# Attention with a gated convolution: two narrow score blocks in one run, and half-width products sorted by width

## The chip, the cores and the metric

One core of one Trainium2 chip runs the kernel. The metric is the device time of one execution in microseconds (us). Over three runs the kernel before takes 2233.45 to 2233.79 us, with a median of 2233.68 us.

## The reference

Eight batches, each with 3200 rows; `u` and `v` have 256 columns, `z` has 64.

```python
scores = scale * np.matmul(z, z.transpose(0, 2, 1))     # scale = 1/3200
attn = np.maximum(scores, 0.0) ** 2
x = u * np.matmul(attn, v)
gate_pre = sum(conv_w[k] * xp[:, k:k + S, :] for k in range(5))   # causal, per channel
out = (1 / (1 + np.exp(-gate_pre)) * (x @ w_val)) @ w_out
```

The score matrix is symmetric: query and key are both `z`. So a block of scores, once computed, serves a second time when it is turned over.

## The kernel before

**Precision.** Every matrix product is made of three products of 32-bit "r" operands: each operand is split into a high part and a low remainder, and high x low, low x high and high x high are summed in PSUM. For the attention weights the high part is a tile `ah` (a cast, on ACT nearly everywhere) and the remainder a tile `al` (a subtraction, on DVE). There are four buffers of each.

**Side by side.** All large products contract over 64 rows at a time: the upper and the lower half of TensorE's rows each get a list of matmuls, and `side_by_side` (L421 to L433) issues one from each list in turn. The text calls two such matmuls a *pair*. A pair with 512 moving columns is called wide, one with 256 narrow.

**Tiles and steps.** A batch has 25 tiles of 128 rows. As queries they form six chunks of four tiles (c = 0 to 5) and one last single tile, called ONE; as keys they form 12 pairs of tiles and a single one, `SINGLE`. A *step* is one chunk of queries against one pair of keys, so that chunks 0 to 4 have 13 steps (positions 0 to 12) and chunk 5, into which the three steps of ONE are mixed, has 16. A step's key pair is *computed* (scores by TensorE, then on ACT a relu, L651, and a square, L652) or *fetched*: read back from DRAM, where an earlier chunk has stored the turned block. `MIRRORED_AT` fixes at which positions the fetched ones stand. With `F` fetched, `c` computed, `1` the single key tile and `H` the block that is half computed and half fetched, the positions of batches 1 to 7 are

```
chunk 0  ccccccccccc1H        chunk 3  cFccFcFcF1FHF
chunk 1  ccccFcccFcc1H        chunk 4  cFccFFFFFF1FH
chunk 2  ccccFcFcFcF1H        chunk 5  1FcFFSFFFSFHSFFF   (S is a step of ONE; batch 7: 1FcSFSFSHFFFFFFF)
```

In batch 0 only chunks 2 to 5 have an `H`.

**The order on TensorE** is written out by hand in the main loop. In each step s it issues: the first half of the step's attention product (`attend(..., 0)`, six wide pairs, three for the single key tile); then the scores of the step three later (`AHEAD = 3`), if these are computed; then what `filling` has for the step; and then the second half (`attend(..., 1)`). Between the two halves the two row halves swap their accumulators. If a step has neither scores nor filling, its second half is put off (`left`) until a step that has some: then all the second halves that were put off follow one another. `lacks(s)` says that there are no scores for the step three later. A computed block of 512 queries and two key tiles is three wide pairs. The single key tile (`1`) and the half block (`H`) are three narrow pairs each, in a PSUM buffer of their own (`s0` and `s1`, taken in turn by `s_bank`).

**Weights.** At the end of step s, `weights_of` (L609 to L672) issues relu, square and cast on ACT and the subtraction on DVE for step s + 3; for `H` these are L625, L626, L632 and L637, for the others L651, L652, L655 and L663. The new `ah` and `al` take the buffers of step s - 1, so they wait for that step's second half.

**ONE's products.** For the last single tile of queries the roles are swapped (`swap_list`): the weights are stationary and `v` moves. For each of the 25 key tiles there is one wide pair (`ah` against both parts of `v`) and one narrow pair (`al` against the high part). Steps S carry eight key tiles each, issued in two pieces of eight pairs, in the step itself and in the next one; K, the `1` of chunk 5, carries one. The pieces go through `filling`.

Of the kernel before, what the change touches and what calls it, by code (L numbers as in the profile page):

```python
# [12 lines left out]
P = 128  # L13
# [4 lines left out]
def attn_glu_kernel(  # L18
# [40 lines left out]
    n_chunks = NT // 4  # L59
    ONE = n_chunks  # L60
    sizes = [4] * n_chunks + [1]
    firsts = [4 * c for c in range(n_chunks + 1)]
    homes = [(c, t) for c, n in enumerate(sizes) for t in range(n)]
    CW = 4 * P
# [3 lines left out]
    AHEAD = 3  # L68
# [198 lines left out]
    def tiles(c, i):  # L267

        return (GROUP * i, GROUP) if c == ONE else pairs[i]

    def two_pairs(b, c):

        return c < n_chunks and (b > 0 or c > 1)

    def own(c, x):
        return 2 * c + x

    SINGLE = NP - 1
# [12 lines left out]
    def mirrored(b, c, i):  # L291
        k, n = tiles(c, i)
        return all(keeps(b, homes[t][0], c) for t in range(k, k + n))
# [8 lines left out]
    steps, starts = [], {}  # L302
# [26 lines left out]
    N = len(steps)  # L329
# [94 lines left out]
    def side_by_side(upper, lower):  # L424


        ins = None
        for i in range(max(len(upper), len(lower))):
            for r, mms in zip(rows, (upper, lower)):
                if i < len(mms):  # L430
                    out_, st, mv, first, last = mms[i]
                    ins = nc.tensor.matmul(out_, st[r], mv[r], start=first, stop=last)  # L432
        return ins  # L433
# [22 lines left out]
    st_, at = {}, {}  # L456
# [14 lines left out]
    def scores(b, c, i, terms=range(3)):  # L471
        if not terms:
            return
        k, n = tiles(c, i)
        w = sizes[c] * P
        if (b, c, i) not in st_:
            st_[b, c, i] = s_bank()
            if b == c == i == 0:
                apart0.append(ps.tile([P, 512], F32, name="acc1", bufs=1))
        s = st_[b, c, i]  # L480

        q = zt[b, c]
        if halves(b, c, i):
            q, w = q[:, :, w // 2 :], w // 2
        if both(c, i):
            q, w = z_last[b], w + P
        each = w // 2 if n == 1 else w
        sides = []
        for j in range(2):
            g, t = homes[k + (0 if n == 1 else j)]  # L490
            ks = slice(t * P, (t + 1) * P)
            qs = slice(j * each, (j + 1) * each) if n == 1 else slice(0, each)
            kk = zt[b, g]
            mms = []
            for m in terms:
                kp, qp = (((0, 0), (0, 1), (1, 0)) if b == c == i == 0 else ((0, 1), (1, 0), (0, 0)))[m]
                bank = apart0[0] if b == c == i == 0 and j else s[:, j]
                mms.append((bank[:, :each], kk[:, kp, ks], q[:, qp, qs], m == 0, m == 2))
            sides.append(mms)
        side_by_side(*sides)  # L500

    def both(c, i):
        return c == n_chunks - 1 and i == SINGLE
# [7 lines left out]
    def halves(b, c, i):  # L511
        return two_pairs(b, c) and i == own(c, 1)
# [189 lines left out]
    def swap_list(b, c, i, bank):  # L702

        if b not in swaps:
            held_s[0] = next_s[0]
            swaps[b] = ps.tile([P, 2, 512], F32, name=f"s{held_s[0]}", bufs=1)
            swapped[b] = 0
        out_ = swaps[b][:, bank]
        if c == ONE:
            k, n = tiles(c, i)  # L710
            ah, al = (x[:, : n * P].rearrange("p (j x) -> p j x", j=n) for x in at[b, c, i])
        else:
            k, n, w = NT - 1, 1, sizes[c] * P
            ah, al = (x[:, w : w + P].rearrange("p (j x) -> p j x", j=1) for x in at[b, c, i])
        mms = []
        for j in range(n):
            both_v = vt[b, (k + j) // 2][:, :, (k + j) % 2]
            first = swapped[b] + j == 0
            last = swapped[b] + j == NT - 1
            whole = (out_.rearrange("p (x d) -> p x d", x=2), ah[:, j], both_v, first, last)  # L720
            half = (out_[:, :D], al[:, j], both_v[:, 0], False, False)
            mms += [whole, half] if first else [half, whole]
        return mms

    def swap(b, c, i, piece=0, pieces=1):

# [597 lines left out]

    def lacks(s):

        return s + AHEAD >= N or mirrored(*steps[s + AHEAD])

    PIECES = {
# [27 lines left out]
    def fill_at(s, fn, *args):  # L1357
        filling.setdefault(s, []).append((fn, *args))
# [48 lines left out]
    for b in range(B):  # L1407
        for c in range(n_chunks + 1):
            s0 = start(b, c)
            met = start(b, 0) + firsts[c] // 2 - AHEAD  # L1410
            if b == 0:
                met -= c == 1
                at_step(-AHEAD - 4 if c == 2 else met - 5, z_load, b, c)
                if c in (1, 2):
                    at_step(-AHEAD - 2, z_double, b, c)
                early = 1 if c == 0 else -1 if c == 3 else 0
                if c != 1:
                    at_step(met - 3 - early, z_turn, b, c)
                    at_step(met - 2 - early - (c == 3), z_high, b, c)
                    at_step(met - 1 - early - (c >= 2) - (c == 3), z_low, b, c)  # L1420
            else:
                s1 = Z_FROM[b][c] + start(b, 0)
                at_step(s1, z_load, b, c)
                late = 1 if b == 1 else 0
                at_step(s1 + late + 3, z_turn, b, c)
                at_step(s1 + late + 4, z_high, b, c)
                at_step(s1 + late + 5, z_low, b, c)
            if c == ONE:
                continue
            nxt = start(*divmod(b * n_chunks + c + 1, n_chunks))  # L1430
            nb, nc_ = divmod(b * n_chunks + c + 1, n_chunks)
            for h in range(DH):
                for part in range(2):
                    at_step(max(s0 + U_LOAD[b > 0][c], 2) + 2 * h + part, u_load, b, c, h, part)
            if (b, c) != LAST:
                for r, fn, args in BEHIND:
                    r -= b == c == 0 and fn is x_low
                    late = b == c == 0 and fn in (gate_value, gate_value_high, gate_value_low)
                    if late:
                        r = min(r + FIRST_VALUE - VALUE, FIRST_LAST[r])  # L1440
                        if fn is not gate_value_low and args == (1,):
                            r, args = (r - 1, (1, "zz")) if fn is gate_value else (r - 1, args)
                    elif fn in (gate_value, gate_value_high, gate_value_low):
                        r = GATE.get(max(value_places(nb, nc_), default=VALUE), {}).get(r, r)
                    at_step(nxt + r, fn, b, c, *args)
                ends = project_places(nb, nc_)
                for x in range(DH):
                    at_step(nxt + (2 if len(ends) > 1 else project_at(nb, nc_) + 1 + x), out_copy_before, b, c, x)
                if b or c:
                    at_step(nxt + 5, out_unpark, *divmod(b * n_chunks + c - 1, n_chunks))  # L1450
            at_step(max(s0 + U_PREP[b > 0][c], 6), u_prep, b, c)
        for s in range(start(b, 0), start(b + 1, 0)):
            if mirrored(*steps[s]) or halves(*steps[s]):
                sooner = steps[s][:2] == (0, n_chunks - 2)
                at_step(s - AHEAD - FETCH - sooner, m_fetch, *steps[s], first=True)
            if steps[s][1] == ONE:
                for piece in range(2):
                    fill_at(s + piece, swap, *steps[s], piece, 2)
                done = s + 1
            elif both(*steps[s][1:]):  # L1460
                fill_at(s, swap, *steps[s])
        if b < B - 1:
            at_step(done, one_take, b)
        else:
            at_step(done + 1, one_take, b, first=True)
        if b == 0:
            for i in (2, *range(4, NP)):
                at_step(i - 3 + (i == 2), v_high, b, i)
                at_step(i - 2, v_low, b, i)
            for k in (0, 2, 4, 6, 24):  # L1470
                at_step(k // 2 - (5 if k else 7), v_load0, k)
            for g in range(2, 6):
                at_step(firsts[g] // 2 - 5, v_load_chunk, b, g)
        else:
            s1 = start(b - 1, n_chunks - 1)
            for i, p in enumerate(V_HIGH):
                p += b == 1 and p > 13
                at_step(s1 + p, v_high, b, i)
                at_step(s1 + p + 1, v_low, b, i)
            for p, tiles_, place_ in V_LOAD:  # L1480
                p += b == 1 and p > 13
                at_step(s1 + p, v_load_at, b, tiles_, place_)
# [245 lines left out]
```

## Time and profile before

| | |
|---|---|
| median of three runs | 2233.68 us |
| the profiled execution's own time | 2233.61 us |
| its span, first to last instruction | 2231.8 us |
| TensorE (PE) busy | 2227.0 us, 100% of the span, 20083 matmuls |
| VectorE (DVE) busy | 1862.1 us, 83% |
| ScalarE (ACT) busy | 1659.5 us, 74% |
| granted TensorE clock, mean | 1.00 of 2.4 GHz |
| narrow pairs of `H` and `1` scores and of ONE's products | 3 pairs a block; 200 pairs |

The first table of the page gives each engine's busy time. Matmuls overlap in it (a 512-column matmul is shown with 387 ns, while pairs start every 227 ns), so what a run of matmuls costs is read from starts in the timeline: from the start of its first pair to the start of the first pair behind it.

### The profile page before, as it was taken

What the parts mean: (1) busy time and instruction counts of PE and PEld (TensorE: products, weight loads), DVE (VectorE), ACT (ScalarE), POOL (GpSimd) and SP (SyncE); (2) the same over time, 40 slices, a digit from 0 to 9 for tenths busy, and PEclk for the clock granted to TensorE, in tenths of its full rate; (3) what the DMA queues carried; (4) which work ended last, traced back from release to release, by engine and by line L of the source; (5) the groups of instructions that cost most, each with busy time, mean ns of one, the idle gap of its engine ahead of it and who ended that gap; (6) DMA issues with size and microseconds to landing.
All of it is one profiled execution on the core that took longest, in us unless ns stands there. A gap on an engine that the chain in (4) does not pass through costs nothing.

```text
span 2231.8 us, 49169 instructions
## 1 busy us (share of the span) xinstructions
PE 2227.0 (100%) x20083; PEld 1886.7 (85%) x20083; DVE 1862.1 (83%) x2307; ACT 1659.5 (74%) x2038; POOL 87.0 (4%) x131
## 2 busy tenths in 40 slices
PE   9999999999999999999999999999999999999999
PEld 8888888888888888888888888888888888888888
DVE  8978798877888778887889868888788987888777
ACT  8886688766887668876688766877668776687764
POOL 0000000000000000000000000000000000000001
PEclk9999999999999999999999999999999999999999
DMA  6568767886678866788577885778858787587763
GB/s 154 123 143 203 205 154 169 183 200 183 158 171 188 202 176 156 177 190 200 162 177 171 189 207 152 174 177 185 211 145 186 175 185 204 149 182 176 168 179 110
DMA packets 707859, 390.34 MB, mean 175 GB/s; under 512 B 419120, under 2 KB 641328, under 8 KB 707632
## 3 DMA queue, kind: packets, MB, share of 16 engines
q1 hardware_dynamic: 707056, 386.74, 71.6%
q8 instruction: 157, 2.57, 0.5%
q14 instruction: 70, 0.57, 0.1%
q10 hardware_dynamic: 576, 0.46, 0.1%
HBM read 213.53 MB, written 173.54 MB: 173 GB/s over the span
## 4 chain that ended last, share of the span: by engine, by line
PE 95%; ACT 2%; DVE 2%; issue 1%; POOL 0%; DVEq 0%; ACTq 0%; POOLq 0%
PE acc L432 69%; PE s L432 13%; PE misc L432 12%; ACT a L652 1%; DVE turned L524 1%; ACT a L651 1%; PE acc L752 0%; ACT ah L655 0%; DVE al L663 0%; PE acc L747 0%; PE misc L747 0%; PE s L883 0%; PE misc L990 0%; DVE gate L830 0%; PE misc L439 0%
## 5 line engine op out<-in xcount | busy, mean ns | idle before, releaser
L432 PE MATMUL acc<-ah,v_hl 64*128 64x512 f32 x9288 | 1546.4, 387 | 0.0
L432 PEld LDWEIGHTS acc<-ah,v_hl 64*128 64x128 f32 x9288 | 889.3, 184 | 162.3 <-issue 0.3
L432 PE MATMUL acc<-al,v_hl 64*128 64x512 f32 x4644 | 915.6, 387 | 0.1
L663 DVE TENSOR_TENSOR al<-a,ah 128x1024 fp32r<-128x1024 f32 x342 | 392.3, 1147 | 160.1 <-ACT ah L655 159.4
L432 PEld LDWEIGHTS acc<-al,v_hl 64*128 64x128 f32 x4644 | 445.1, 184 | 80.2 <-DVE al L663 1.1
L651 ACT ACTIVATE a<-s 128x1024 f32<-128x1024 f32 x342 | 329.5, 963 | 136.5 <-PE s L432 117.1
L655 ACT CAST ah<-m 128x1024 fp32r<-128x1024 f32 x256 | 266.7, 1045 | 161.4 <-PE acc L432 97.0
L652 ACT ACTIVATE a<-a 128x1024 f32<-128x1024 f32 x342 | 343.5, 1004 | 10.9
L663 DVE TENSOR_TENSOR al<-m,ah 128x1024 fp32r<-128x1024 f32 x256 | 310.1, 1211 | 33.9 <-ACT ah L655 33.9
L524 DVE STREAM_TRANSPOSE turned<-a 128x1024 f32<-128x1024 f32 (+1 forms) x282 | 323.5, 1147 | 0.8 <-DMA mir<-turned 0.8
L655 ACT CAST ah<-a 128x1024 fp32r<-128x1024 f32 (+2 forms) x317 | 313.8, 990 | 13.5 <-PE acc L432 3.5
L830 DVE SCALAR_TENSOR_TENSOR gate<-x,cw,gate 128x512 f32<-128x512 f32 (+1 forms) x392 | 285.5, 728 | 4.4 <-ACT gate L828 0.5
L432 PE MATMUL s<-zhl,zhl 64*128 64x512 f32 x996 | 140.9, 387 | 0.0
L782 DVE TENSOR_TENSOR x<-acc,ut 128x512 f32<-128x512 f32 (+1 forms) x94 | 60.1, 681 | 75.0 <-PE acc L432 68.9
L933 ACT CAST gvh<-gv 128x512 fp32r<-128x512 f32 x94 | 58.4, 621 | 81.1 <-DVE gv L929 81.0
L432 PEld LDWEIGHTS s<-zhl,zhl 64*128 64x128 f32 x996 | 95.5, 184 | 17.4 <-DVE zhl L258 0.3
L834 ACT ACTIVATE gate<-gate 128x512 f32<-128x512 f32 (+1 forms) x98 | 61.0, 622 | 62.1 <-DVE gate L830 61.8
L432 PE MATMUL s<-zhl,zhl_last 64*128 64x512 f32 (+1 forms) x720 | 88.7, 350 | 0.0
L929 DVE TENSOR_TENSOR gv<-misc,gate 128x512 f32<-128x512 f32 x92 | 63.2, 687 | 21.3 <-PE misc L432 17.1
L432 PEld LDWEIGHTS s<-zhl,zhl_last 64*128 64x128 f32 x720 | 66.1, 184 | 11.1
L432 PE MATMUL s<-v_hl,ah 64*128 64x512 f32 x400 | 73.2, 395 | 0.0
L432 PE MATMUL misc<-xh,w_val_lo 64*128 64x512 f32 x368 | 72.3, 386 | 0.0
(245 smaller groups left out, 2099.7 us busy)
## 6 DMA issues: line engine op xcount, KB each, us to landing
mir<-turned SPq DMA_DIRECT2D x468, 256.0 KB, 4.1
m<-mir SPq DMA_DIRECT2D x234, 512.0 KB, 4.9
u_raw<-in_u_dram SPq DMA_DIRECT2D x384, 64.0 KB, 3.6
mir<-turned SPq DMA_DIRECT2D x376, 64.0 KB, 2.2
m<-mir SPq DMA_DIRECT2D x94, 256.0 KB, 4.3
out_dram<-ob SPq DMA_DIRECT2D x180, 128.0 KB, 3.0
v_raws<-in_v_dram SPq DMA_DIRECT2D x25, 512.0 KB, 5.8
z_raw<-in_z_dram SPq DMA_DIRECT2D x180, 64.0 KB, 3.4
```

The lines of the kernel that those rows point to most:

```text
L432: ins = nc.tensor.matmul(out_, st[r], mv[r], start=first, stop=last)
L524: nc.vector.transpose(into[:, t : t + m], src)
L651: nc.scalar.activation(to, src, AF.Relu, scale=scale)
L652: nc.scalar.activation(a, a, AF.Square)
L655: nc.scalar.copy(hi, a)
L663: nc.vector.tensor_tensor(lo, a, f32(hi), op=ALU.subtract)
L782: nc.vector.tensor_tensor(x[:, h, HALO + cols.start : HALO + cols.stop], accs[b, c][h][:, cols] if with_ is None else with_, ut[b, c][:, h ...
L830: nc.vector.scalar_tensor_tensor(g, tap, cw[:, h, k : k + 1], g, op0=ALU.mult, op1=ALU.add)
L834: nc.scalar.activation(g, g, AF.Sigmoid)
L929: nc.vector.tensor_tensor(gv[:, :w], pvs[b, c][e][:, :w], gates[b, c][:, e, :w], op=ALU.mult)
L933: nc.scalar.copy(gvs[b, c][0][:, e, :w], gv_[b, c, e][:, :w])
```

## The change

Three edits.

First, where a chunk has both a `1` and an `H` and is not the last of its batch, `scores` for the `1` now takes one PSUM buffer for both: the `1` fills columns 0 to 255 of its two banks, the `H` columns 256 to 511, and the six narrow pairs are issued in one run, at the place of the `1`. The later step, in which the `H` scores stood, has no scores any more; `lacks` says so, and by the rule above it puts its second half off, if nothing else fills it.

Second, `swap_list` returns all the narrow pairs of a step of ONE ahead of all its wide ones (the other way round for the first step of a batch), where they alternated. As `cut` halves the list, the first piece is then eight narrow pairs and the second eight wide ones.

Third, a step of ONE issues its two pieces one step sooner if the scores that stand in that sooner step are those of an `H`. By the orders above that is the step at position 9 of chunk 5 in batches 0 to 6.

```diff
-        s = st_[b, c, i]
-
+        sides = score_lists(b, c, i, st_[b, c, i], terms)
+        if joined(b, c, i):
+            st_[b, c, own(c, 1)] = st_[b, c, i][:, :, CW // 2 :]
+            for mms, more in zip(sides, score_lists(b, c, own(c, 1), st_[b, c, own(c, 1)], terms)):
+                mms += more
+        side_by_side(*sides)
+
+    def joined(b, c, i):
+        return i == SINGLE and c < n_chunks - 1 and two_pairs(b, c)
...
-            mms += [whole, half] if first else [half, whole]
-        return mms
+            wholes.append(whole)
+            halves.append(half)
+        return wholes + halves if swapped[b] == 0 else halves + wholes
...
-        return s + AHEAD >= N or mirrored(*steps[s + AHEAD])
+        if s + AHEAD >= N:
+            return True
+        b, c, i = steps[s + AHEAD]
+        return mirrored(b, c, i) or (halves(b, c, i) and c < n_chunks - 1)
...
+                sooner = halves(*steps[s - 1 + AHEAD])
                 for piece in range(2):
-                    fill_at(s + piece, swap, *steps[s], piece, 2)
+                    fill_at(s + piece - sooner, swap, *steps[s], piece, 2)
```

(`score_lists` holds what `scores` did before: it makes the two lists of matmuls for one block.)

## Rows read from the trace of the kernel before

**Rows 1.** Page: span; busy us of each engine, share, instructions.
```profile
span 2231.8 us, 49169 instructions
PE 2227.0 (100%) x20083; PEld 1886.7 (85%) x20083; DVE 1862.1 (83%) x2307; ACT 1659.5 (74%) x2038; POOL 87.0 (4%) x131
```
**Rows 2.** Waits of PE: who waited for whom, total us, times, longest.
```profile
PE misc L439 <- POOL zeros L1525: 1.1, 1, 1.1
```
**Rows 3.** Timeline, PE, batch 3, chunk 3: start us, us, instructions merged.
```profile
1003.01 0.53 PE L432 MATMUL s<-zhl 64*128 64x256 f32 x6
...
1008.15 0.86 PE L432 MATMUL s<-zhl 64*128 64x512 f32 x6
1008.83 0.40 PE L432 MATMUL acc<-ah,v_hl 64*128 64x512 f32 x2
```
**Rows 4.** Timeline, PE: six narrow pairs, then five wide ones.
```profile
1283.47 0.28 PE L432 MATMUL misc<-w_out_hi,one_r 64*128 64x256 f32 x2
...
1284.18 0.40 PE L432 MATMUL acc<-ah,v_hl 64*128 64x512 f32 x2
...
1285.34 0.62 PE L432 MATMUL acc<-ah,v_hl 64*128 64x512 f32 x4
```
**Rows 5.** Timeline, PE: twelve narrow pairs, then scores.
```profile
103.45 0.28 PE L432 MATMUL misc<-w_out_hi,gvl 64*128 64x256 f32 x2
...
104.88 0.86 PE L432 MATMUL s<-zhl,zhl 64*128 64x512 f32 x6
```
**Rows 6.** Timeline, PE, batch 3, chunk 5: a piece of eight alternating pairs.
```profile
1088.52 0.28 PE L432 MATMUL s<-v_hl,al 64*128 64x256 f32 x2
...
1089.92 0.40 PE L432 MATMUL acc<-ah,v_hl 64*128 64x512 f32 x2
...
1091.30 0.28 PE L432 MATMUL s<-v_hl,al 64*128 64x256 f32 x2
```
**Rows 7.** Groups by line and shape: count, busy us, mean ns, idle before.
```profile
L432 PE MATMUL s<-v_hl,al 64*128 64x256 f32 x400 | 56.7, 277 | 0.0
```
**Rows 8.** Timeline, DVE, batch 3, chunk 3, up to the subtraction of position 10.
```profile
987.72 1.23 DVE L663 TENSOR_TENSOR al<-a,ah 128x1024 fp32r<-128x1024 f32 x1 [1.87 <-ACT ah L655]
...
1002.90 0.71 DVE L830 SCALAR_TENSOR_TENSOR gate<-x,cw,gate 128x512 f32<-128x512 f32 x1
1003.52 1.22 DVE L663 TENSOR_TENSOR al<-m,ah 128x1024 fp32r<-128x1024 f32 x1
```
**Rows 9.** Timeline, batch 2, chunk 2: a subtraction that ends late.
```profile
663.90 1.18 DVE L663 TENSOR_TENSOR al<-m,ah 128x1024 fp32r<-128x1024 f32 x1
...
665.14 0.19 PEld L432 LDWEIGHTS acc<-al,v_hl 64*128 64x128 f32 x2 [0.20 <-DVE al L663]
...
665.47 0.63 PE L432 MATMUL acc<-ah,v_hl 64*128 64x512 f32 x4
```
**Rows 10.** Timeline, batch 2, chunk 3: subtraction of position 10, scores of step 10.
```profile
727.31 1.22 DVE L663 TENSOR_TENSOR al<-m,ah 128x1024 fp32r<-128x1024 f32 x1
...
733.37 0.84 PE L432 MATMUL s<-zhl 64*128 64x512 f32 x6
```
**Rows 11.** Timeline, batch 1, chunk 0: subtraction of position 10, scores of step 10.
```profile
318.80 1.23 DVE L663 TENSOR_TENSOR al<-a,ah 128x1024 fp32r<-128x1024 f32 x1 [0.21 <-ACT ah L655]
...
322.52 0.84 PE L432 MATMUL s<-zhl 64*128 64x512 f32 x6
```
**Rows 12.** Timeline, batch 3, chunk 3, ACT and DVE: weights of positions 11 and 12.
```profile
1005.33 0.60 ACT L632 CAST ah<-m 128x512 fp32r<-128x512 f32 x1
...
1006.88 1.05 ACT L655 CAST ah<-m 128x1024 fp32r<-128x1024 f32 x1
...
1007.96 1.22 DVE L663 TENSOR_TENSOR al<-m,ah 128x1024 fp32r<-128x1024 f32 x1 [0.62 <-ACT ah L655]
```
**Rows 13.** Timeline, batch 3, chunk 5: subtraction of position 12 and its use.
```profile
1092.28 1.22 DVE L663 TENSOR_TENSOR al<-m,ah 128x1024 fp32r<-128x1024 f32 x1
...
1095.45 0.28 PE L432 MATMUL s<-v_hl,al 64*128 64x256 f32 x2
```

More of the change, by code (lines that the diff above doesn't have):

```diff
@@ L473, in scores @@
             return
-        k, n = tiles(c, i)
-        w = sizes[c] * P
         if (b, c, i) not in st_:
@@ L479, in scores, with score_lists @@
                 apart0.append(ps.tile([P, 512], F32, name="acc1", bufs=1))
-        s = st_[b, c, i]
+        sides = score_lists(b, c, i, st_[b, c, i], terms)
[6 more added lines that the diff above has]
+        return i == SINGLE and c < n_chunks - 1 and two_pairs(b, c)
+    def score_lists(b, c, i, s, terms):
+        k, n = tiles(c, i)
+        w = sizes[c] * P
         q = zt[b, c]
@@ L499, in scores @@
             sides.append(mms)
-        side_by_side(*sides)
+        return sides
     def both(c, i):
@@ L714, in swap_list @@
             ah, al = (x[:, w : w + P].rearrange("p (j x) -> p j x", j=1) for x in at[b, c, i])
-        mms = []
+        wholes, halves = [], []
         for j in range(n):
```

## The prediction

> **What bounds the kernel now.** I read the page first: TensorE is busy for 2227.0 of 2231.8 us [rows 1], and its list of waits has one entry, 1.1 us at the start [rows 2]. So the time is the sum of TensorE's issue times, and a change counts only as far as it makes matmuls issue closer or brings a wait. The other engines matter only through the instant at which they deliver. Next I read the timeline by start times, since busy times of matmuls overlap. A wide pair takes 0.227 us: three from 1008.15 to 1008.83 [rows 3]. At the same rate a narrow one would take 0.113.
>
> **Price of a narrow run.** From 1003.01 to 1008.15 [rows 3] the order of the code puts three narrow pairs and 21 wide ones: second halves of positions 7 and 8 (6 + 6), first halves of 9 and 10 (3 + 6). At the two rates that is 0.34 + 4.76 = 5.10; the rows show 5.14, so a block of three costs 0.04 more than its columns. Where does this sit? Six narrow pairs take 0.71 (1283.47 to 1284.18) against 0.68, 0.03 more, and the five wide ones behind them 1.16 against 1.13, another 0.03 [rows 4]: so a narrow run pays a little in each pair and about 0.03 once, when it goes back to wide. Twelve take 1.43 us, 0.119 each [rows 5]: 0.006 per narrow pair, not growing. A run of three is then 0.02 + 0.03, a bit over what rows 3 show; I take 0.04 for three and 0.006 for each pair beyond. Eight pairs that alternate, with the six wide ones behind, take 2.78 (1088.52 to 1091.30) against 4 x 0.113 + 10 x 0.227 = 2.72: 0.06 for a piece [rows 6].
>
> **The change, part by part.**
>
> *Joining.* Batch 0 joins in chunks 2 to 4, batches 1 to 7 in chunks 0 to 4: 3 + 35 = 38 joins. Two blocks cost 2 x 0.04, one run of six 0.04 + 3 x 0.006 = 0.06. Saved: 0.02 each, **0.7 us** in all (bounds 0.4 to 1.1 by the 0.01 us of the rows).
>
> *Sorting.* 400 narrow matmuls are 200 pairs, 25 a batch [rows 7]; one is in K, whose order stays, and 24 in three steps S, 24 steps in all. Before, a step pays 2 x 0.06 = 0.12. After, a piece of eight narrow pairs pays 0.04 + 5 x 0.006 = 0.07 and a piece of eight wide ones nothing. Saved: 0.05 each, 1.2 us. In eight of them the narrow piece now stands right behind the narrow `H` scores (seven by the sooner step; in batch 7 it stood there already), so one return to wide goes too: 8 x 0.03 = 0.2. Together **1.4 us** (bounds 1.0 to 1.8).
>
> *What costs nothing.* The number and shape of all instructions stay, also of relu, square, cast and subtraction; no DMA is issued elsewhere, so SP's and POOL's queues keep their order, and nothing is moved past them. Buffers alternate as before, with one turn fewer; a joined buffer is next written at the second computed block behind it, two steps or more after the relu of its `H` is issued.
>
> *What comes late.* This is the other side of the account. A second half that is put off lets the next first halves come sooner, and these need their `ah` and `al`. In chunks 0, 1, 2 and 4 one second half (position 9 or, in chunk 4, 8 and 9 together) goes behind the scores of step 10, and position 10's first half comes 1.36 us sooner. In chunk 3 of batches 1 to 7 position 8 now has no scores, position 9 never had any, so the second halves of 7 and 8, 12 pairs, go behind the scores of step 10: position 10 is wanted 2.72 us sooner. (The three narrow pairs that move from step 8 to step 6 cancel.) In batch 3 its first half starts six pairs ahead of the scores of step 10, at 1008.15 - 1.36 = 1006.79 [rows 3]; after, at 1004.07 on the same clock. Its `al` is ready at 1003.52 + 1.22 = 1004.74 [rows 8]. That is 0.67 us too late. Can DVE be sooner? Its last idle time is at 987.72, behind it follow 17 us without a gap [rows 8], and nothing in the change lightens them. What does a late `al` cost? In batch 2 one ends at 663.90 + 1.18 = 665.08; the weight load that waited starts at 665.14 and the pair behind it at 665.47 [rows 9]. From the `al` to that pair are 0.39 us. On time, it would start two pairs after the first of the block, which needs no `al`: 0.45. So 0.06 us of lateness is free, and batch 3 loses 0.61 us here. Batches 1, 3 and 5 have the same order; in 2, 4 and 6 the work of ONE's groups stands in between, and in batch 2 the same `al` ends at 728.53 while its first half starts at 733.37 - 1.36 = 732.01 [rows 10]: 3.48 us of room, 0.76 left. Batch 7 has as much. So 3 x 0.61 = **1.8 us** lost. In the other chunks I looked for less than 1.36 us of room at position 10: batch 1, chunk 0, where `al` ends at 320.03 and is wanted at 322.52 - 1.36 = 321.16 [rows 11]: 0.23 late, 0.17 lost. Sum of stalls **2.0 us** (0 if the casts and subtractions come sooner than on this trace, 4 if as late again).
>
> *The sooner step and the pieces.* ONE's narrow pairs need `al`; position 9's is issued at the end of step 6 and now used in step 8, behind a first half and the `H` scores, which I take as no cost. At position 12, `al` ends at 1093.50 and is used at 1095.45 [rows 13]. Position 10's second half (1.36) now goes behind that use, and the sorting takes about 0.1 more: 0.5 us of room left, no cost; if DVE there is 0.5 us later, it costs what is beyond.
>
> *Sum.* 2233.6 (profiled execution) - 0.7 - 1.4 + 2.0 = **2233.5 us**. The median of the runs shown is 0.07 above the profiled one, so I leave it at that. The gain in issue is given back as waits for DVE.
>
> A rule weighed. Rows 6 and 3 show that a piece of alternating widths costs 0.06 us more than its columns. The Trainium skill, "TensorE: Matmul & The Clock Gate", section "Back-to-back issue gap", gives an isolated warm matmul N / 2.4 + 2.5 ns, by its own columns alone; by that the order of widths would be free and both savings nothing. The trace disagrees, with 2.78 against 2.72 us. What it would make of the time is the case of the free order below.
>
> **The rivals.**
> - *No stall* (the weights come in time): 2233.6 - 2.1 = 2231.5. For it: the slack is 0.7 us in 13 steps' work, and relu and square of `H` can run sooner. Against it: DVE had no gap for 17 us [rows 8].
> - *Slower: the four `ah` buffers run out.* At step 10 of chunk 3 the second halves of 7, 8, 9 and 10 are all open, so positions 11 and 12 wait for theirs. Their casts began at 1005.33 and 1006.88, the latter's subtraction ended at 1009.18 [rows 12]. Pushed by 2.72, less what they had spare, position 12 ends near 1011.5 and is wanted near 1012.2 (one first half behind 11's, which follows 1008.15 by 2.72). Room: 0.7 us. If a buffer is seen as free only one second half (1.36) later, position 12 is 0.6 us late and 11 about 0.1, in batches 1, 3 and 5: 3 x 0.7 = 2.1 more, 2235.6. It decides from 0.7 us of extra delay on.
> - *The order of widths is free*: 2233.6 + 2.0 = 2235.6. Against it stand rows 3 to 6.
> - *The change doesn't do what it says*, if the relu of the `1` has to wait for the `H` in the same buffer: 0.35 us on ACT in 38 places. In chunk 3 the cast of position 10 follows it, but DVE is busy until 1003.52 anyway; elsewhere a few tenths: 2234.
>
> **How the numbers follow.** Forecast 0.5 (2233.5, own range 2232.5 to 2234.5); no stall 0.2 (2231.5); buffers run out 0.17 (2235.6); free order 0.05 (2235.6); late relu 0.08 (2234). A range from 2231.0 to 2235.7 leaves out the tails of the second and third case and holds 8 in 10. A measurement of this kernel tells 0.2%, 4.5 us, from no change. Every case lies within this; only several together go beyond, stalls of twice the size and buffers on one side, savings above their bounds on the other: faster 0.04, same 0.90, slower 0.06.
>
> **What would show it.** In the list of waits TensorE stays near 1 us, but in batches 1, 3 and 5 weight loads `acc<-al` wait for DVE L663 by some 0.6 us, at the first half of chunk 3's position 10, after step 8 has lost its scores. Runs of six narrow score pairs take 0.71 us; ONE's pieces become 0.95 (narrow) and 1.82 (wide) where both took 1.40. On ACT the casts L632 of chunk 3 start about 2.7 us later. It would be wrong if the same stall appears in batches 2, 4 and 6, if position 12 of chunk 3 or of chunk 5 waits, or if the time leaves 2231.0 to 2235.7.

## The result: 0.5% slower, and outside the range

The changed kernel takes 2245.51 us (median of 6 runs, 2243.92 to 2247.08) against 2233.56 us before (6 runs, 2233.20 to 2233.79) on the same chip: ratio 1.0054, 95% interval [1.0043, 1.0064]. The forecast was 2233.5. The profiled execution took 2244.64 us. All lines named below as after's are those of the changed kernel: its L672, L939 and L948 are L663, L929 and L938 before.

The page after, beside [rows 1]: the number of matmuls is the same, and TensorE is 14 us short of its span, where it was 4.8 us short.

```profile
span 2242.9 us, 49210 instructions
...
PE 2228.9 (99%) x20083; PEld 1940.9 (87%) x20083; DVE 1862.9 (83%) x2307; ACT 1658.6 (74%) x2038; POOL 87.2 (4%) x131
```

The waits of TensorE after (who waited for whom, total us, times, longest), beside the single entry of [rows 2]:

```profile
PE misc L432 <- DVE gv L939: 7.2, 4, 1.9
PE misc L439 <- POOL zeros L1539: 1.1, 1, 1.1
PE acc L432 <- DVE al L672: 1.0, 3, 0.3
PE acc L432 <- DVE al L583: 0.8, 1, 0.8
```

Two entries count. `acc <- al`, three times, is the stall that was predicted. `misc <- gv`, four times, is one that the prediction does not have. (`acc <- al` L583 stands at 10.03 us, in the start-up.) The same two stand in the list of the weight loads, which sit in front of the matmuls. It shows a stall in its full length; of the ten waits for `al` three are these, 0.77 us each, and the others are 0.15 to 0.45.

```profile
PEld misc L432 <- DVE gv L939: 8.5, 4, 2.2
PEld acc L432 <- DVE al L672: 4.0, 10, 0.8
```

**The predicted stall**, timeline after, batch 3, chunk 3 (start us, us, engine, line, what; in brackets the idle time and what ended it), beside [rows 8]:

```profile
1006.51 1.22 DVE L672 TENSOR_TENSOR al<-m,ah 128x1024 fp32r<-128x1024 f32 x1
...
1007.78 0.19 PEld L432 LDWEIGHTS acc<-al,v_hl 64*128 64x128 f32 x2 [0.77 <-DVE al L672]
1007.78 0.51 PE L432 MATMUL acc<-al,v_hl 64*128 64x512 f32 x2 [0.34 <-DVE al L672]
1008.12 0.64 PE L432 MATMUL acc<-ah,v_hl 64*128 64x512 f32 x4
```

`al` ends at 1007.73 and the weight load that waited starts 0.05 us later; the pair behind it follows 0.39 after the `al`, as [rows 9] had it.

**The other stall**, the same view after, batch 2, chunk 3:

```profile
728.35 1.22 DVE L672 TENSOR_TENSOR al<-m,ah 128x1024 fp32r<-128x1024 f32 x1
...
728.67 0.39 PE L432 MATMUL acc<-ah,v_hl 64*128 64x512 f32 x2
728.90 0.27 PE L432 MATMUL misc<-w_out_hi,one_r 64*128 64x256 f32 x1
...
729.49 0.69 DVE L948 TENSOR_TENSOR gvl<-gv,gvh 128x512 fp32r<-128x512 f32 x1
730.28 0.69 DVE L939 TENSOR_TENSOR gv<-misc,gate 128x512 f32<-128x512 f32 x1
...
731.03 0.18 PEld L432 LDWEIGHTS misc<-w_out_hi,one_r 64*128 64x128 f32 x1 [2.17 <-DVE gv L939]
731.03 0.38 PE L432 MATMUL misc<-w_out_hi,one_r 64*128 64x256 f32 x1 [1.86 <-DVE gv L939]
731.03 0.50 PE L432 MATMUL misc<-w_out_lo,one_r 64*128 64x256 f32 x2
```

and before:

```profile
729.24 0.69 DVE L929 TENSOR_TENSOR gv<-misc,gate 128x512 f32<-128x512 f32 x1
...
730.59 0.28 PE L432 MATMUL misc<-w_out_hi,one_r 64*128 64x256 f32 x2
```

This is ONE's group product (`one_project`), filled in at position 9 of chunk 3. It writes banks named `misc`; DVE's `gv` multiplication first has to read what the value product of chunk 2, which is issued in chunk 3, left in one of them. One matmul goes out at 728.90, the next waits until `gv` has ended at 730.97. Before, `gv` ended at 729.93 and the product started at 730.59: 0.66 us of room that no list of waits shows. The 12 pairs of positions 7 and 8, put off past the product, bring it 12 x 0.227 = 2.72 us forward: 2.06 too late, and 0.06 from the end of `gv` to the matmul make 2.12. The product resumes 731.03 - 728.90 = 2.13 after it began.

**The clock.** In batch 4 the same stall ends at 1286.23. Busy time by stretch, of batch 4 and then of batch 2 (us; busy us and count per engine; granted clock, DMA share, GB/s):

```profile
core 0: us, PE busy (x) PEld busy (x) DVE busy (x) ACT busy (x) POOL busy (x), PEclk, DMA share, GB/s
1284.20:1286.20 2.00, 0.17 (x3) 0.00 (x0) 1.87 (x3) 1.22 (x3) 0.62 (x1) 1.00 1.21 241
1286.50:1289.80 3.30, 3.30 (x23) 3.30 (x23) 0.00 (x0) 0.00 (x0) 0.00 (x0) 0.50 0.55 116
1289.90:1293.00 3.10, 3.10 (x30) 3.10 (x29) 1.48 (x3) 2.61 (x4) 0.00 (x0) 1.00 1.17 206
...
729.00:731.00 2.00, 0.17 (x3) 0.00 (x0) 1.87 (x3) 1.22 (x3) 0.62 (x1) 1.00 1.19 294
731.10:734.40 3.30, 3.30 (x35) 3.30 (x37) 0.32 (x1) 0.97 (x2) 0.00 (x0) 1.00 0.79 139
```

Behind the stall of batch 4 TensorE gets 0.50, 1.2 of 2.4 GHz, throughout these 3.3 us and has 23 matmuls in them; behind that of batch 2, of the same length, it keeps 1.00 and has 35. The clock's own records have 0.50 from 1286.45, 0.2 us after the stall's end, to 1289.87. Half of these 3.4 us is 1.7, an estimate of the loss; by the starts of the chunks it is 1.6. The mean clock of the six runs is 0.997 to 0.999, and the times spread over 3.2 us where those before spread over 0.6.

**The ledger**, how much later each chunk starts than before in the two profiled executions: chunk 3 of batches 1, 3 and 5 adds 0.66, 0.67 and 0.63; of batches 2, 6 and 7 2.10, 2.11 and 1.89; of batch 4 3.71, which is 2.1 and the clock. Start-up adds 0.68, batch 1 chunk 0 0.23, and all the rest, sorting and joining in the main, takes back 1.7. Sum 11.0: 2233.61 to 2244.64.

### The profile page after: what moved, and what is told of

It is laid out like the page before. It is cut to its first block, busy times and chain, and to the rows that moved or that the text cites. A ratio compares the mean times of both kernels' runs of the same rounds, so it can differ in the third digit from the quotient of the medians.

```text
span 2242.9 us, 49210 instructions
## 1 busy us (share of the span) xinstructions
PE 2228.9 (99%) x20083; PEld 1940.9 (87%) x20083; DVE 1862.9 (83%) x2307; ACT 1658.6 (74%) x2038; POOL 87.2 (4%) x131
## 4 chain that ended last, share of the span: by engine, by line
PE 92%; DVE 4%; DMA 1%; issue 1%; ACT 1%; SPq 1%; DVEq 0%
PE acc L432 65%; PE s L432 13%; PE misc L432 12%; DVE al L672 1%; DVE turned L533 1%; DMA mir<-turned 1%; DVE gate L840 1%; PE acc L762 0%; SPq L557 0%; DVE ut L781 0%; PE acc L757 0%; PE misc L757 0%; DVE gv L939 0%; DMA v_raw<-in_v_dram 0%; DMA out_dram<-ob 0%
## 5 line engine op out<-in xcount | busy, mean ns | idle before, releaser
L432 PEld LDWEIGHTS acc<-ah,v_hl 64*128 64x128 f32 x9288 | 928.6, 184 | 137.9 <-issue 0.5
L432 PE MATMUL acc<-al,v_hl 64*128 64x512 f32 x4644 | 940.1, 387 | 1.9 <-DVE al L672 1.0
L432 PEld LDWEIGHTS acc<-al,v_hl 64*128 64x128 f32 x4644 | 469.0, 184 | 72.1 <-DVE al L672 4.0
L672 DVE TENSOR_TENSOR al<-a,ah 128x1024 fp32r<-128x1024 f32 x342 | 392.1, 1146 | 148.2 <-ACT ah L664 146.4
L672 DVE TENSOR_TENSOR al<-m,ah 128x1024 fp32r<-128x1024 f32 x256 | 309.8, 1210 | 32.7 <-ACT ah L664 32.7
L646 DVE TENSOR_TENSOR al<-m,ah 128x512 fp32r<-128x512 f32 x46 | 31.8, 692 | 69.9 <-ACT ah L641 69.1
L939 DVE TENSOR_TENSOR gv<-misc,gate 128x512 f32<-128x512 f32 x92 | 63.2, 687 | 22.0 <-PE misc L432 17.8
```

The lines of the kernel that those rows point to most:

```text
L646: nc.vector.tensor_tensor(l, src, f32(h), op=ALU.subtract)
L672: nc.vector.tensor_tensor(lo, a, f32(hi), op=ALU.subtract)
L939: nc.vector.tensor_tensor(gv[:, :w], pvs[b, c][e][:, :w], gates[b, c][:, e, :w], op=ALU.mult)
```

## Experiments

Two theories besides the waits (W): that a join costs by itself, in the long narrow run or the shared buffer (J); that the sorting or the sooner step costs (S). Beside the first four runs the kernel before takes 2233.56 us, beside the next four 2233.40, beside the last 2233.47; ratios are to these.

**Sorting and sooner step without the joins**

```
 def joined(b, c, i):
-    return i == SINGLE and c < n_chunks - 1 and two_pairs(b, c)
+    return False
...
-    return mirrored(b, c, i) or (halves(b, c, i) and c < n_chunks - 1)
+    return mirrored(b, c, i)
```

> Only the sorting and the sooner step; no block is joined, and no second half is put off. Theory W (the loss is in waits that the put-off second halves of chunk 3 bring: in batches 2, 4, 6 and 7 ONE's output product comes before DVE has read the banks it writes, about 2 us each; in 1, 3 and 5 the al of position 10 is late, 0.65 us each): no such wait, and the issue time saved stays, 2233.6 - 1.4 = 2232.2 us. Theory S (the sorted pieces or the sooner step cost): 2234 or more. Theory J (the joined run or its shared buffer costs): 2232.2 as well.

Measured: 2231.84 us (11 runs, 2231.63 to 2232.36) against 2233.56, ratio 0.9993 [0.9984, 1.0001]. No wait of TensorE is left but the start:

```profile
PE misc L439 <- POOL zeros L1539: 1.1, 1, 1.1
```

By the starts of the chunks batches 0 to 6 gain 0.18 to 0.25 us each in their sorted chunk 5, and differ by at most 0.04 in the other chunks (start-up apart). Batch 7, in which no step comes sooner, gains 0.20 by the end of its last step S, so the gain does not need the sooner step. S falls. The interval of the time alone reaches 1.0001; it is the chunks that show the gain.

**Joins alone, order and step as before**

```
-            wholes.append(whole)
-            halves.append(half)
-        return wholes + halves if swapped[b] == 0 else halves + wholes
+            mms += [whole, half] if first else [half, whole]
+        return mms
...
-                    fill_at(s + piece - sooner, swap, *steps[s], piece, 2)
+                    fill_at(s + piece, swap, *steps[s], piece, 2)
```

> Only the joining, with ONE's products alternating and at their old steps. W: all the waits of the change stay and 1.4 us of issue time come back, 2245.5 + 1.4 = 2246.9 us. J: the same, 2247. S: near 2233.

Measured: 2246.55 us (5 runs, 2244.99 to 2246.97), 1.0056 [1.0042, 1.0070]. The whole loss is in the joins, and its waits are those of the whole change:

```profile
PE misc L432 <- DVE gv L938: 7.2, 4, 1.9
...
PE acc L432 <- DVE al L672: 1.0, 3, 0.4
```

**The whole change, chunk 3 of batches 1 to 7 not joined (31 joins stay)**

```
-    return i == SINGLE and c < n_chunks - 1 and two_pairs(b, c)
+    return i == SINGLE and c < n_chunks - 1 and two_pairs(b, c) and not (b and c == 3)
...
-    return mirrored(b, c, i) or (halves(b, c, i) and c < n_chunks - 1)
+    return mirrored(b, c, i) or (halves(b, c, i) and c < n_chunks - 1 and not (b and c == 3))
```

> The whole change, but chunk 3 of batches 1 to 7 keeps its two blocks apart: 31 joins instead of 38. W: all waits of chunk 3 go, the 0.25 us of batch 1, chunk 0 stay: 2233.6 - 1.4 - 31 x 0.02 + 0.25 = 2231.8 us, and the spread between runs goes back to some 0.6 us. J: the loss goes with the number of joins, 31/38 of 12 us less the savings: about 2243. S: 2244.

Measured: 2231.80 us (11 runs, 2231.56 to 2231.87), 0.9992 [0.9983, 1.0001]. All of the loss hangs on seven of the 38 joins; the other 31 have the same shared buffer and the same runs of six. By the starts of the chunks they lose 0.26 us in batch 1 chunk 0, where the prediction had its small stall, and gain 0.02 in most others. J falls.

**The kernel before, nothing joined or sorted, only the second halves put off in chunk 3**

```
+    put_off = bool(ahead) and b > 0 and ahead[1] == 3 and halves(*ahead)
-    if terms or fill or behind or s + 1 == WHOLE_FROM:
+    if (terms and not put_off) or fill or behind or s + 1 == WHOLE_FROM:
```

> The kernel before, with nothing joined or sorted; in chunk 3 of batches 1 to 7 the H scores stay at their own step, but the second halves that followed them there are put off as in the change. W: the same waits come without any joined block: 4 x 2.1 + 3 x 0.65 = 10.4, with 0 to 4 falls of the clock of up to 1.7 us each: 2244 to 2250 us. J and S: 2233.6, unchanged.

Measured: 2246.72 us (5 runs, 2243.69 to 2246.95), 1.0055 [1.0043, 1.0068]:

```profile
PE misc L432 <- DVE gv L929: 6.8, 4, 1.8
...
PE acc L432 <- DVE al L663: 1.0, 3, 0.3
```

Here the scores stay where they were; only the order of second halves is that of the change. The loss comes from the putting off. Its five runs also show the clock: 2243.69 at a mean of 1.0, 2245.09 at 0.999, the other three, near 2246.9, at 0.998. Without a fall the stalls cost 2243.69 - 2233.56 = 10.1 us, and each fall 1.4 to 1.8 more.

**The change, second halves no longer put off: flushed at step 8 without cover, in all 38 chunks or in the seven**

```
+    free = bool(ahead) and ahead[1] < n_chunks - 1 and halves(*ahead)
-    if terms or fill or behind or s + 1 == WHOLE_FROM:
+    if terms or fill or behind or free or s + 1 == WHOLE_FROM:
```

(for the seven, `free` asks for `b > 0 and ahead[1] == 3` in place of `ahead[1] < n_chunks - 1`)

> The whole change, but in all 38 places the second halves are not put off: they follow at the step that has lost its H scores, with nothing between the two halves (the accumulators change hands bare). W: no wait for DVE, not even in batch 1, chunk 0; what is left is the price t of a bare turn: 2231.84 - 38 x 0.02 = 2231.1 plus 38 t; with t from 0 to 0.3 us 2231 to 2242. J: 2245.

> The whole change, but only in chunk 3 of batches 1 to 7 the second halves follow at step 8 with a bare turn. W: the waits of chunk 3 go, all 38 joins stay: 2231.84 - 0.76 + 0.25 (batch 1, chunk 0) = 2231.3 plus 7 t: 2231.3 to 2233.4. J: 2245.

Measured: all 38, 2245.41 us (5 runs, 2245.36 to 2245.50), 1.0054 [1.0041, 1.0066]; the seven, 2234.16 (11 runs, 2233.87 to 2234.29), 1.0003 [0.9995, 1.0012]. J had 2245 for both; the first comes to it, but for another reason, and the second, with all its 38 joins, does not. No matmul waits for `gv` or for the `al` of chunk 3 any more; the weight loads wait for TensorE's own matmuls instead, 38 and 7 times:

```profile
PEld acc L432 <- PE acc L432: 18.4, 38, 0.5
```

```profile
PEld acc L432 <- PE acc L432: 3.4, 7, 0.5
```

One of the seven, timeline, batch 3:

```profile
1003.01 0.95 PE L432 MATMUL acc<-ah,v_hl 64*128 64x512 f32 x4
1003.46 0.19 PEld L432 LDWEIGHTS acc<-ah,v_hl 64*128 64x128 f32 x2 [0.49 <-PE acc L432]
...
1003.80 0.40 PE L432 MATMUL acc<-al,v_hl 64*128 64x512 f32 x2
```

From the first of these rows to the last are two pairs, 0.45 us by the rate of a wide pair, and 0.79 in the rows: turning from first to second halves with nothing between them costs 0.34 here, and each flushed chunk is 0.32 to 0.37 longer than before. The code asks for this wait: the two row halves swap their banks, and `turn_round` opens the second halves with a wait for the last matmul of the first. So the narrow scores that the join takes out of step 8 were cover for this turn, 0.35 us of work. Both times lie above their expected ranges, which took at most 0.3 for a turn. Flushing in all 38 comes to the same time as the change by another way: no stall, clock 1.0, runs within 0.14 us.

**ONE's product one step later**

```
-            fill_at(s0 + 48 + part, one_project, g, part)
-        at_step(s0 + 49, one_out, g)
+            fill_at(s0 + 49 + part, one_project, g, part)
+        at_step(s0 + 50, one_out, g)
```

> The whole change, with the output product of ONE's groups, its copy and its store one step later (positions 10 and 11 of chunk 3 instead of 9 and 10). W: the four waits for gv go, since the product now stands behind the put-off second halves; but batches 2, 4, 6 and 7 then have at position 10 the order of the odd ones, nothing in between, so that al is late there too: 2231.3 + 7 x 0.65 = 2235.8 us, no fall of the clock. J: 2245.

Measured: 2235.88 us (11 runs, 2235.67 to 2236.09), 1.0011 [1.0002, 1.0020]. That is 2.5 us over the kernel before, where the change is 12.0 over the one beside it. The waits for `gv` are gone, and what was hidden behind them comes up: batches 2, 4 and 6 now stall for `al` as 1, 3 and 5 do (0.61 to 0.64 by the starts of the chunks), and batch 7 loses 0.39.

```profile
PE acc L432 <- DVE al L672: 2.1, 6, 0.4
```

**DVE lightened by one subtraction ahead of chunk 3's weights**

```
-    nc.vector.tensor_tensor(both[:, 1, :w], z_turned.pop((b, c))[:, :w], f32(both[:, 0, :w]), op=ALU.subtract)
+    engine = nc.gpsimd if b > 1 and c == 2 else nc.vector
+    engine.tensor_tensor(both[:, 1, :w], z_turned.pop((b, c))[:, :w], f32(both[:, 0, :w]), op=ALU.subtract)
```

> The whole change, with one subtraction of 128x512 (the low part of the next batch's z of chunk 2, some 0.6 us of DVE's unbroken work in chunk 3 of batches 1 to 6) on GpSimd instead of DVE. W, with DVE's backlog as what is late: in these six the waits shrink by that 0.6 us: al from 0.65 to near 0 in batches 1, 3, 5, gv from 2.1 to 1.5 in 2, 4, 6; batch 7 stays; together 3.7 us off: 2241 to 2243. If DVE's order waits for something else (an ACT cast, a DMA) and not for its own throughput: 2245.5, unchanged.

Measured: 2242.48 us (5 runs, 2240.98 to 2242.81), 1.0040 [1.0026, 1.0053]. Timeline, batch 2, chunk 3:

```profile
725.00 0.69 DVE L673 TENSOR_TENSOR al<-a,ah 128x512 fp32r<-128x512 f32 x1 [0.28 <-ACT ah L665]
...
727.64 0.27 PE L433 MATMUL misc<-w_out_hi,one_r 64*128 64x256 f32 x1
...
728.79 0.69 DVE L940 TENSOR_TENSOR gv<-misc,gate 128x512 f32<-128x512 f32 x1
...
729.54 0.38 PE L433 MATMUL misc<-w_out_hi,one_r 64*128 64x256 f32 x1 [1.63 <-DVE gv L940]
```

One subtraction of 0.69 us less, and the stall shrinks by 0.23 only (1.86 to 1.63), since DVE now waits 0.28 us for a cast on ACT. Batch 6 shrinks by the same 0.23, and the stalls for `al` by as much (weight loads from 0.77 to 0.54). So what is late is DVE's queue, and it can be moved by little before ACT is what is late. Batch 7 shows the same in the change itself: no batch follows it, so DVE lacks this subtraction and the transpose ahead of it, waits 0.87 us for the same cast, and the stall is 1.63. In batch 4 the stall grows to 1.98. There `gv` starts 0.46 us after the instruction ahead of it, where it starts 0.10 after it in batch 2; ACT, named in the row, had ended 0.38 sooner, and what delayed it stays open:

```profile
1283.78 0.69 DVE L940 TENSOR_TENSOR gv<-misc,gate 128x512 f32<-128x512 f32 x1 [0.46 <-ACT a L636]
```

The time lies in the expected range, but not by the expected sum, which had 0.6 in each of six chunks. The two profiled executions lie 3.7 apart. By the starts of the chunks 1.2 of it is in batches 1, 2, 3, 5 and 6, 1.5 in batch 4, where the clock did not fall, and 1.0 in start-up.

**The change, joined only where there was room (27 joins)**

```
 def joined(b, c, i):
-    return i == SINGLE and c < n_chunks - 1 and two_pairs(b, c)
+    return i == SINGLE and c < n_chunks - 1 and two_pairs(b, c) and room(b, c)
+
+def room(b, c):
+    return b == 0 or (c != 3 and (b, c) != (1, 0) and not (c == 2 and b in (2, 4, 6)))
...
-    return mirrored(b, c, i) or (halves(b, c, i) and c < n_chunks - 1)
+    return mirrored(b, c, i) or (halves(b, c, i) and c < n_chunks - 1 and room(b, c))
```

> The whole change, but the two narrow blocks are joined only in the 27 chunks in which the runs so far showed room: not in chunk 3 of batches 1 to 7, not in batch 1 chunk 0 and not in chunk 2 of batches 2, 4 and 6. Theory W (what a join costs is the wait that its missing cover brings, and nothing else): no wait of TensorE for al or gv is left in the trace, each of the 27 joins saves 0.02 us of the sorted kernel without joins (2231.84 us), so about 2231.3 us, and it is the shortest of the versions. Rival (a join has a cost of its own, hidden in e3 by the sorting's gain): 27 joins come to no less than 2231.84 us.

Measured: 2231.52 us (11 runs, 2231.17 to 2232.35) against 2233.47 beside it, 0.9992 [0.9983, 1.0001]; TensorE's waits hold only the start.

```profile
PE misc L439 <- POOL zeros L1542: 1.1, 1, 1.1
```

Against the sorted kernel without joins 26 of the 27 joined chunks are shorter by the starts of the chunks, most of them by 0.02 us, and together 0.53 for 0.54 expected, so the saving of a join is real. By the time it is not shown: the two lie 1.95 and 1.72 us under the kernel before, 0.23 apart, and start-up alone differs by 0.26 between their profiled executions. It is the shortest median of all versions, and its gain of 0.1% is less than this measurement can tell from none.

## Why the prediction was wrong

**What bounds the kernel**: right. The time is TensorE's issue, and the loss shows as idle time on it and, in batch 4, as a lower clock.

**Joining, 38 x 0.02**: right in its size, 0.53 in the 27 chunks of the last experiment. The joined run of batch 3 takes 0.72 us where 0.71 was predicted, beside [rows 4]:

```profile
1001.54 0.52 PE L432 MATMUL s<-zhl,zhl_last 64*128 64x256 f32 x6
1001.90 0.53 PE L432 MATMUL s<-zhl 64*128 64x256 f32 x6
1002.26 0.40 PE L432 MATMUL acc<-ah,v_hl 64*128 64x512 f32 x2
```

**Sorting, 1.4**: right. Sorted alone, a batch gains 0.18 to 0.25, 1.6 in all eight for 1.4. The pieces of batch 3, chunk 5 after, beside [rows 6]:

```profile
1090.33 0.52 PE L432 MATMUL s<-zhl_last 64*128 64x256 f32 x6
1090.68 1.12 PE L432 MATMUL s<-v_hl,al 64*128 64x256 f32 x16
1091.64 0.40 PE L432 MATMUL acc<-ah,v_hl 64*128 64x512 f32 x2
...
1093.03 1.98 PE L432 MATMUL s<-v_hl,ah 64*128 64x512 f32 x16
1094.85 0.39 PE L432 MATMUL acc<-ah,v_hl 64*128 64x512 f32 x2
```

0.96 for the narrow piece and 1.82 for the wide one: predicted 0.95 and 1.82. The order of widths is not free, and that rival falls. The gap of an isolated matmul in the Trainium skill ("TensorE: Matmul & The Clock Gate", "Back-to-back issue gap"), by which the sorting would have gained nothing, does not carry over to these pairs.

**What comes late: this step failed, in batches 2, 4, 6 and 7.** Its method held where it was used: the stalls in batches 1, 3 and 5 stand at the predicted place, and their chunks come out 0.63 to 0.67 longer for 0.61, and batch 1 chunk 0 0.23 for 0.17. But it asked of position 10 alone whether its `ah` and `al` come in time. ONE's product was counted as "work in between", which gives the weights time; that the product is itself brought forward by the same 2.72 us, and what it has to wait for, was not asked. It had 0.66 us of room, and a wait for `gv` of 1.63 to 1.87 us stands there four times, some 8 us of the loss by the ledger, without the clock. Joining only outside chunk 3 gives the time that the sum has without those stalls; putting off alone, with nothing joined, gives the loss.

**What was left out besides: the clock.** The prediction has no price for a long idle time beyond its length. In batch 4 it was 1.6 us more, and in the profiled executions of the joins alone and of the putting off alone it falls behind two stalls, those of batches 2 and 4.

**Rivals.** "No stall" is refuted for the change; its sum fits the kernel with chunk 3 left out, 2231.80 for 2231.5. "Buffers run out": half of it occurred. In chunk 3 of all seven batches the cast of position 11 waits on ACT 2.8 to 4.7 us for second halves to free its buffer, where it did not wait before [rows 12]. But TensorE had no wait for it. In batch 3 the `al` of position 12 ends at 1015.21 and is used at 1016.12, 0.9 us of room for the 0.7 predicted:

```profile
1011.34 0.62 ACT L641 CAST ah<-m 128x512 fp32r<-128x512 f32 x1 [2.93 <-PE acc L432]
...
1013.98 1.23 DVE L672 TENSOR_TENSOR al<-m,ah 128x1024 fp32r<-128x1024 f32 x1 [0.70 <-ACT ah L664]
...
1016.12 0.39 PE L432 MATMUL acc<-al,v_hl 64*128 64x512 f32 x2
```

"Late relu": in batch 3 the narrow block's relu begins at 1004.18 before and at 1007.16 after, 2.98 later in a chunk that starts 3.0 later; not late.

**What would show it wrong**: "if the same stall appears in batches 2, 4 and 6" named the right batches, but for `al`; the list of waits shows `gv` there. The casts of chunk 3 came 3.0 us later on the chunk's own clock (1005.33 to 1011.34, less 3.0), the predicted 2.7 and part of the stall.

## To carry to other kernels

When work is put off, everything between its old and its new place comes sooner, products of other stages too: list each instruction of that stretch and ask of it every condition it has, its operands and also who must first have read the bank that it overwrites. The room of each stands in the trace as the distance from the end of its last releaser to its start; a list of waits shows nothing of it until it is negative. Work that is saved may have been cover: before taking it out, look for the turn or the wait that it hid.

## What the runs showed of the hardware

- Turning from first to second halves, that is to other accumulators for the two row halves, with the wait that the code puts there, costs 0.34 us in the rows of this kernel when nothing stands in between; with three narrow score pairs in between the weight loads show no such wait.
- Behind idle times of 1.3 to 2.0 us on TensorE the granted clock falls to 0.50, for 3.4 us, in some places and not in others: behind one of four in the profiled execution of the change, two of four in those of the joins alone and of the putting off alone, none in that of the lightened DVE. The five falls stand behind stalls of 1.85 to 1.87 us and begin 0.2 to 1.3 us after TensorE has resumed; a stall of 1.98 us had none. Behind stalls of 0.3 us it never fell.
- Behind such a stall the two row halves no longer start together. In batch 2 the two matmuls of a wide pair start 0.003 us apart ahead of it and 0.117 behind it, about the length of a narrow pair, so that groups of four that show 0.62 us show 0.73. The rate stays: three wide pairs still take 0.68 (734.93 to 735.61). Chunk 4 behind such a chunk 3 comes out 0.02 to 0.04 longer than before, where it is 0.02 to 0.05 shorter in batches 1, 3 and 5; that the offset is the cause is not shown.
